# A fused attention, Fourier-mixing and expert kernel: raw weights loaded early, first factors on VectorE, a 127-row store cut in two, a list asked for later

## The chip, the cores and the metric

The kernel runs on one core of a Trainium2 chip. The metric is the device time of one execution in microseconds (us), from launch to end. The kernel before takes 1034.43 us, the median of 3 runs (1032.81 to 1038.68).

## The reference

The inputs are q, k, v of 4 sequences, 8 heads, 576 positions and 64 columns, and the weights of two later stages.

```
attn = softmax(q k^T / 8 - slope_h * |i - j|), only for 0 <= i - j < 128;  x = attn v -> (4, 576, 512)
u    = x + Re(FFT over the positions and over the 512 columns of x)
un   = (u - mean(u)) / sqrt(var(u) + 1e-6);  x2 = u + relu(un @ w_ch1) @ w_ch2      (512 -> 2048 -> 512)
each token of x2 picks an expert (argmax of a gate; a local gate may hand on the expert of the token before)
out  = p[e] * (relu(x2 @ w1[e]) @ w2[e])                                             (8 experts, 512 -> 1024 -> 512)
```

The two weights `w_ch1` and `w_ch2` are handed in as 64-bit floating-point words. The kernel reads them as pairs of 32-bit words and turns them into fp32 itself.

## The kernel before

All tokens lie in 18 groups of 128 rows (five to a sequence, the last one shared by two sequences). Every product of the two-layer networks is done in three fp32r matmuls (helper `mm3`, lines 161 to 164), with both factors split into a high and a low part: `split` (lines 157 to 159) copies the high part on ScalarE (ACT, line 158) and subtracts for the low part on VectorE (DVE) or GpSimd (POOL) (line 159).

The stages overlap on TensorE (PE):

- **Opening**, `opening()`: the attention of sequence 0, its Fourier mixing (`mixing(0)`) and the normalising of the first two groups, in an order written out by hand for PE, DVE, ACT and POOL.
- **First pass** over the first 1024 of the 2048 hidden columns (`mlp_first`, nine pairs of groups), with the attention and the mixing of sequences 1 to 3 beside it. Their pieces are laid on a time axis as lanes; behind that the framework's scheduler sets the order of each engine by its own estimates. Each engine, and SyncE's queue of DMAs (SP), then runs strictly in that order.
- **Second pass** over the other 1024 hidden columns, with the routing of tokens beside it (`route`, `assign`); during its last two pairs an early expert is begun for the 256 first tokens of the expert that leads so far (`early()`, `expert_weights(-1, e)`).
- **Experts**, eight of them, to the end.

`mixing(b)` ends in three steps. The first adds into `xs[0]` (lines 485 to 489) and stores two tiles to the DRAM tiles `ud`: 128 rows at line 492 and 127 rows at line 493 (the row that is left out comes in the third step, line 498). Lines 495, 496, 501 and 502 store the other rows. The tiles `xs` are a ring of four: the attention of a later sequence writes into them at line 401 when these stores have read them. `normalise` loads the groups back from `ud` (`u`, line 553), takes mean and variance on DVE (lines 558 and 560), works out 1/sqrt(var) in 12 tiny steps on POOL (lines 565 to 573: a power, then two Newton steps), scales on ACT (line 577), transposes on PE (line 511) and splits.

The weights of the two passes are converted chunk by chunk: a chunk is 256 hidden columns, in four raw pieces of 512 KB. `load_weights64` and `convert` take a raw piece `r` from a ring of two buffers (`RB = 2`, tag `r64`), load it on SP (line 228), scale it on ACT (line 232), put the words together in three DVE instructions (lines 233 to 235), and split. Four chunks belong to the first pass, four to the second. The third piece of a chunk thus waits in SP's queue until the first is converted.

In `early()`, the list of token slots (`ids`, line 981) is asked for one step after the first expert weights (`we`, line 940, also a ring of two `r64` buffers); it must wait until the last scatter into `slots` (POOL, line 867) has landed.

Of the kernel before, what the change touches and what calls it, by code (L numbers as in the profile page):

```python
# [52 lines left out]
TB_ = 3  # L53
WB = 3
FL = 2
EY = 8
EL = 7
HB = 4
VL = 3
# [91 lines left out]
def build(ctx, tc, a, out):  # L151
# [55 lines left out]
    def weight_tiles(wp):  # L207
        return (wp.tile([P, 2, 4, CB], F32R, tag="w1", name="t1"), wp.tile([P, 2, CB // P, DM], F32R, tag="w2", name="t2"))

    def load_weights64(tiles, w1, w2, c, words):  # L210
        t1, t2 = tiles
        q = CB // 2
        for j in range(2):
            f0 = c * CB + j * q
            s = w1[:, 2 * f0:2 * (f0 + q)].rearrange("(k p) f -> p k f", p=P)
            convert(t1[:, 0, :, j * q:(j + 1) * q], t1[:, 1, :, j * q:(j + 1) * q], s, words)
            yield
        for j in range(CB // P):
            f0 = c * CB + j * P
            s = w2[f0:f0 + P].rearrange("p (k f) -> p k f", k=4)  # L220
            convert(t2[:, 0, j].rearrange("p (k f) -> p k f", k=4), t2[:, 1, j].rearrange("p (k f) -> p k f", k=4), s, words)
            yield

    def convert(hi, lo, src, words):

        k, n = hi.shape[1], hi.shape[2]
        r = wraw.tile([P, k, 2 * n], U32, tag="r64", name="r64", bufs=RB)
        nc.sync.dma_start(out=r, in_=src)
        w = r.rearrange("p k (n t) -> p k n t", t=2)
        wl, y = w[:, :, :, 0], w[:, :, :, 1]  # L230
        t = words().rearrange("p (k n) -> p k n", k=k)
# [194 lines left out]
    def mixing(b):  # L426
        xs = xss.pop(b)
        rows = [(P, P), (P, P), (33, 32)]
        zin = []

        def fold(kt):
            n, m = rows[kt]
            xa, xb = xs[kt][:, 0], xs[kt][:, 1]
            xf = slab([P, 2, DM], F32, "xf", "m", MB)
            xe, xo = xf[:, 0], xf[:, 1]
            if kt == 0:

# [12 lines left out]
        zn = sm.tile([1, K1], F32, tag="tmp", name="zn", bufs=1)  # L450
        parts = ((1, 0), (1, 1), (0, 0)), ((0, 1), (0, 2))
        pss = {}

        def zprod(part, kt):
            xf, n = zin[kt]
            for cs, db in part:
                w = P if db < 2 else 1
                if kt == 0:
                    pss[cs, db] = ps_g.tile([P, DM], F32, tag="g", name="zps")
                nc.tensor.matmul(pss[cs, db][0:w, 0:K1], lhsT=xf[0:n, cs, db * P:db * P + w], rhs=tab1[0:n, cs, kt], start=kt == 0, stop=kt == 2)  # L460
                if kt == 2:
                    nc.scalar.copy(Z[cs][:, db] if db < 2 else zn, pss.pop((cs, db))[0:w, 0:K1])

        for kt in range(3):
            fold(kt)
            zprod(parts[0], kt)
            yield
        for kt in range(3):
            zprod(parts[1], kt)
        yield  # L470
        for kb in range(3):
            n = rows[kb][0]
            c0 = kb * P
            pc = ps_g.tile([P, DM], F32, tag="g", name="pc")
            pz = ps_g.tile([P, DM], F32, tag="g", name="pz")
            for cs, ps in ((1, pz), (0, pc)):
                for db in range(2):
                    nc.tensor.matmul(ps[0:n, 0:K2], lhsT=Z[cs][:, db, c0:c0 + n], rhs=tab2[:, cs, db], start=db == 0, stop=db == 1 and cs == 1)
            nc.tensor.matmul(pc[0:n, 0:K2], lhsT=zn[:, c0:c0 + n], rhs=alt, start=False, stop=True)
            cb_ = slab([P, 3, K2], F32, "cmb", "m", MB)  # L480
            sb, df, su = cb_[:, 0], cb_[:, 1], cb_[:, 2]
            nc.scalar.copy(sb[0:n], pz[0:n, 0:K2])
            nc.vector.tensor_tensor(out=df[0:n], in0=pc[0:n, 0:K2], in1=sb[0:n], op=ALU.subtract)
            nc.vector.tensor_tensor(out=su[0:n], in0=pc[0:n, 0:K2], in1=sb[0:n], op=ALU.add)
            for ab, lo, hi in ((0, df, su), (1, su, df)):
                m = rows[kb][ab]
                x = xs[kb][0:m, ab]
                nc.vector.tensor_tensor(out=x[:, 0:HN + 1], in0=x[:, 0:HN + 1], in1=lo[0:m, 0:HN + 1], op=ALU.add)
                nc.vector.tensor_tensor(out=x[:, DM - 1:HN:-1], in0=x[:, DM - 1:HN:-1], in1=hi[0:m, 1:HN], op=ALU.add)
            row = lambda t: ud[GIDX[b, t]]  # L490
            if kb == 0:
                nc.sync.dma_start(out=row(0), in_=xs[0][:, 0])
                nc.sync.dma_start(out=row(3)[1:P], in_=xs[0][1:P, 1])
            elif kb == 1:
                nc.sync.dma_start(out=row(1), in_=xs[1][:, 0])
                nc.sync.dma_start(out=row(2), in_=xs[1][:, 1])
            else:
# [4 lines left out]
                nc.sync.dma_start(out=um[r + 32:r + 64], in_=xs[2][0:32, 1])  # L502
            if kb == 2:
                mixed[0] = b
            yield
# [40 lines left out]
    def normalise(gs, xT, us, src=None):  # L546
# [15 lines left out]

        v = sm2.tile([P, 3, TM], F32, tag="v", name="v")
        v0, v1, v2 = (v[:, i, 0:n] for i in range(3))
        nc.gpsimd.tensor_scalar_add(v0, mv[:, 0:n, 1], 1.0e-6)
        nc.gpsimd.tensor_tensor(out=v1, in0=v0, in1=half[:, 0:n], op=ALU.pow)
        for _ in range(2):
            nc.gpsimd.tensor_tensor(out=v2, in0=v1, in1=v1, op=ALU.mult)
            nc.gpsimd.tensor_tensor(out=v2, in0=v2, in1=v0, op=ALU.mult)
            nc.gpsimd.tensor_scalar(out=v2, in0=v2, scalar1=-0.5, scalar2=1.5, op0=ALU.mult, op1=ALU.add)  # L570
            nc.gpsimd.tensor_tensor(out=v1, in0=v2, in1=v1, op=ALU.mult)
        nc.gpsimd.tensor_tensor(out=v2, in0=mv[:, 0:n, 0], in1=v1, op=ALU.mult)
        nc.gpsimd.tensor_scalar_mul(v2, v2, -1.0)
        yield
        for i, g in enumerate(gs):
            un = us[i]
# [37 lines left out]
                for _ in pre:  # L614
                    yield ("piece", 0)

    chunksA = [weight_tiles(wpA) for c in range(FA // CB)]
    def tables():

        with tc.issue_after(last["load"].ins):  # L620
# [14 lines left out]

    def conversions():
        for c in range(FA // CB):
            yield from load_weights64(chunksA[c], a["w_ch1"], a["w_ch2"], c, lambda: sm.tile([P, 2 * CB], U32, tag="t64", name="t64", bufs=2))

    END = object()  # L640

# [34 lines left out]
    def opening():  # L676

        for n, _ in enumerate(attention(0)):
            if n == 4:
                tables()  # L680
        attended.add(0)
        ends = [last[x].ins for x in ("x", "w", "pool")]
        xs = xss[0]
# [54 lines left out]
    chunksB = [weight_tiles(wpB) for c in range(FA // CB, FF // CB)]  # L738

    room = lact.tile([P, 4, 2 * CB], U32, tag="xTe", name="t64", bufs=1)  # L740
    turns = iter(range(4 * FF // CB))
    for c in range(FA // CB, FF // CB):
        for _ in load_weights64(chunksB[c - FA // CB], a["w_ch1"], a["w_ch2"], c, lambda: room[:, next(turns) % 4]):
            pass

    wt8 = late.tile([P, E], F32, name="wt8")
# [250 lines left out]
    def early():  # L997

        e = first_expert()
        pre_.add(expert_weights(-1, e))  # L1000
        yield
        x = slot_load(e * CAP, TM, 1)
        for _ in range(EL):
            yield
        ids[-1] = slot_ids(x, TM, 1)
        xTs[-1] = lact.tile([P, 2, 4, TM * P], F32R, tag="xTe", name="xTe", bufs=1)
# [196 lines left out]
```

## Time and profile before

| | |
|---|---|
| median of 3 runs | 1034.43 us |
| profiled execution, its time | 1039.1 us |
| its span, first to last instruction | 1037.4 us |
| PE busy | 946.8 us (91%) |
| DVE, ACT, POOL busy | 520.1, 381.3, 241.1 us |
| mean granted clock of PE | 0.959 |

Busy means that an instruction of the engine was running. The granted clock is the share of full speed that TensorE was allowed; 1.00 is 2.4 GHz and 0.50 is 1.2 GHz. Of the 1037.4 us, PE is idle in 90.6, and it runs at the lower of its two levels in several stretches beside these.

### The profile page before, as it was taken

Reading aid. Unit: us, or ns where it says so; the run is one execution under the profiler, and the core shown is the slowest. Engines: PE = TensorE matmul, PEld = TensorE weight load, DVE = VectorE, ACT = ScalarE, POOL = GpSimd, SP = SyncE. Lnnn points to the kernel's source line nnn. Section 1 sums busy time; section 2 is a strip of 40 time slices with the busy share of each in tenths; the row PEclk is TensorE's granted clock in tenths of the full one; section 3 lists DMA queues with packets and bytes.
Section 4 is the critical chain, followed back from the end, with each engine's and each line's share of the span. In section 5 each row is a group of like instructions: output and inputs, shape, how many; then the busy total and the mean of one; then the engine's idle time right before and its main releaser. Section 6 shows DMA issues by size and latency. Waiting matters only on the chain. (4 is left out here: it accounts for less than half of the span.)

```text
span 1037.4 us, 16275 instructions
## 1 busy us (share of the span) xinstructions
PE 946.8 (91%) x5959; PEld 770.6 (74%) x5959; DVE 520.1 (50%) x1286; ACT 381.3 (37%) x990; POOL 241.1 (23%) x358
## 2 busy tenths in 40 slices
PE   8877989889799888899999999997987999999993
PEld 4636666567568567688988888886876988888993
DVE  5777856636444455611133535354767644555510
ACT  5345654353252233421111111112436644454510
POOL 2245531230222034401011222222122212111100
PEclk9987999899989998999999999999999999999997
DMA  8345841342212155514344444444349745555300
GB/s 301 98 128 158 283 153 43 131 140 69 78 36 63 57 188 166 184 61 102 62 102 102 103 102 102 103 102 122 123 144 302 237 142 183 179 163 183 119 18 18
DMA packets 112103, 133.58 MB, mean 129 GB/s; under 512 B 16253, under 2 KB 79998, under 8 KB 111950
## 3 DMA queue, kind: packets, MB, share of 16 engines
q1 hardware_dynamic: 89166, 112.73, 34.0%
q0 software_dynamic: 22848, 19.72, 8.8%
q8 instruction: 49, 0.80, 0.3%
q14 instruction: 40, 0.33, 0.1%
HBM read 104.08 MB, written 31.23 MB: 130 GB/s over the span
## 5 line engine op out<-in xcount | busy, mean ns | idle before, releaser
L527 ACT ACTIVATE h<-hps 128x256 fp32r<-128x256 f32 x152 | 58.1, 382 | 263.7 <-PE hps L164 257.9
L528 DVE SCALAR_TENSOR_TENSOR h<-hps,h 128x256 fp32r<-128x256 f32 x152 | 63.7, 419 | 173.8 <-ACT h L527 173.5
L162 PE MATMUL acc<-t,h 128*128 128x512 f32 x304 | 127.8, 423 | 7.9 <-ACT h L527 7.0
L163 PE MATMUL acc<-t,h 128*128 128x512 f32 x304 | 123.6, 407 | 0.9 <-POOL t L159 0.8
L164 PE MATMUL acc<-t,h 128*128 128x512 f32 x304 | 120.5, 400 | 0.5 <-DVE h L528 0.5
L159 DVE TENSOR_TENSOR t<-we,t 128x512 fp32r<-128x512 f32 x144 | 93.8, 686 | 53.0 <-ACT t L158 52.3
L158 ACT CAST t<-we 128x512 fp32r<-128x512 f32 x144 | 82.6, 618 | 49.7 <-PE acc L164 24.9
L162 PE MATMUL hps<-xT,t 128*128 128x256 f32 x288 | 87.9, 305 | 4.9 <-DVE h L528 2.8
L162 PE MATMUL hps<-xTe,t 128*128 128x256 f32 (+5 forms) x288 | 87.0, 303 | 2.3 <-ACT xTe L158 2.3
L163 PE MATMUL hps<-xTe,t 128*128 128x256 f32 (+5 forms) x288 | 86.7, 301 | 0.3 <-DVE xTe L159 0.3
L164 PE MATMUL hps<-xTe,t 128*128 128x256 f32 (+5 forms) x288 | 86.9, 302 | 0.0
L164 PE MATMUL hps<-xT,t 128*128 128x256 f32 x288 | 84.4, 293 | 0.2 <-POOL t L159 0.2
L163 PE MATMUL hps<-xT,t 128*128 128x256 f32 x288 | 84.1, 292 | 0.0
L162 PE MATMUL hps<-xTb,t 128*128 128x256 f32 x288 | 83.2, 289 | 0.0
L164 PE MATMUL hps<-xTb,t 128*128 128x256 f32 x288 | 82.6, 287 | 0.0
L163 PE MATMUL hps<-xTb,t 128*128 128x256 f32 x288 | 82.2, 286 | 0.0
L345 ACT ACTIVATE t<-t,mx 128x128 f32<-128x128 f32 (+1 forms) x160 | 62.6, 394 | 47.3 <-DVE mx L338 43.1
L162 PEld LDWEIGHTS acc<-t,h 128*128 128x128 f32 x304 | 58.1, 193 | 25.5 <-ACT h L527 11.9
L162 PEld LDWEIGHTS hps<-xT,t 128*128 128x128 f32 x288 | 57.6, 200 | 16.1 <-DVE h L528 7.6
L162 PE MATMUL acc<-t,hE 128*128 128x512 f32 x168 | 67.6, 402 | 0.1
L164 PEld LDWEIGHTS acc<-t,h 128*128 128x128 f32 x304 | 57.7, 191 | 12.6 <-DVE h L528 1.1
L163 PEld LDWEIGHTS acc<-t,h 128*128 128x128 f32 x304 | 58.8, 194 | 10.3 <-POOL t L159 2.3
(260 smaller groups left out, 2039.8 us busy)
## 6 DMA issues: line engine op xcount, KB each, us to landing
we<-in_w SPq DMA_DIRECT2D x72, 512.0 KB
r<-in_w_ch SPq DMA_DIRECT2D x32, 512.0 KB
qkt<-in_qk SPq DMA_DIRECT2D x15, 642.0 KB
nd<-xT SPq DMA_DIRECT2D x18, 512.0 KB
xTb<-nd POOLq DMA_DIRECT2D x18, 512.0 KB, 6.0
vt<-in_v SPq DMA_DIRECT2D x16, 384.0 KB
pd<-y SPq DMA_DIRECT2D x18, 256.0 KB
ub<-ud SPq DMA_DIRECT2D x18, 256.0 KB
```

The lines of the kernel that those rows point to most:

```text
L158: nc.scalar.copy(hi, src)
L159: (eng or nc.vector).tensor_tensor(out=lo, in0=src, in1=hi.bitcast(F32), op=ALU.subtract)
L162: nc.tensor.matmul(o, lhsT=wh, rhs=xh, start=start, stop=False, **kw)
L163: nc.tensor.matmul(o, lhsT=wh, rhs=xl, start=False, stop=False, **kw)
L164: return nc.tensor.matmul(o, lhsT=wl, rhs=xh, start=False, stop=stop, **kw)
L345: nc.scalar.activation(t[0:m, j], t[0:m, j], AF.Exp, bias=mx[0:m, j:j + 1], scale=-1.0, accum_out=sums[0:m, j:j + 1])
L527: nc.scalar.activation(h[:, 0, 0:n], hps[:, 0:n], AF.Relu)
L528: nc.vector.scalar_tensor_tensor(out=h[:, 1, 0:n], in0=hps[:, 0:n], scalar=0.0, in1=h[:, 0, 0:n].bitcast(F32), op0=ALU.max, op1=ALU.subtract)
```

## The change

Four edits:

1. **Raw weights.** `load_raw` loads the four raw pieces of a chunk into the place of a chunk that is not converted yet (tiles `rw` with the tags `w1` and `w2` of the weights' own pool). Chunks 0 to 2 of each pass go that way, chunk 3 still goes through the ring `r64`. In the opening chunk 0 is asked for after step 9 of the attention, chunks 1 and 2 after step 14; in the second pass chunks 4 to 6 behind the last store to `ud`. A chunk is then converted from its raw tile, into the tile that is free next.
2. **First factors.** Where `normalise` gets its rows from SBUF (only the first pair of groups, in the opening), 1/sqrt is worked out on DVE: a bit-shift first guess and three Newton steps, 17 tiny instructions in place of POOL's 12.
3. **Stores.** The 127-row store becomes one of 112 rows and one of 15.
4. **Early list.** The list `ids` is asked for seven steps later, behind the first weights; it is read two steps after that, and the rows are transposed five (`EY`) and not eight steps after they are gathered: 15 steps in all, 16 before.

```diff
-EY = 8
+EY = 5
...
+    def blocks64(c):
...
+            yield w1[:, 2 * f0:2 * (f0 + q)].rearrange("(k p) f -> p k f", p=P)
...
+            yield w2[f0:f0 + P].rearrange("p (k f) -> p k f", k=4)
+
+    def load_raw(c, wp=None):
+        if wp is not None:
+            raws[c] = [x[:, i] for x in (wp.tile([P, 2, 4, CB], U32, tag=g, name="rw") for g in ("w1", "w2")) for i in range(2)]
+        for i, s in enumerate(blocks64(c)):
+            if wp is None:
+                raws.setdefault(c, []).append(wraw.tile([P, 4, CB], U32, tag="r64", name="r64", bufs=RB))
+            nc.sync.dma_start(out=raws[c][i], in_=s)
+            yield
+
+    def load_weights64(chunks, i, c, wp, words):
+        t1, t2 = chunks[i] = weight_tiles(wp)
+        q = CB // 2
+        late_load = load_raw(c) if c not in raws else iter(())
+        for _ in range(RB - 1):
+            next(late_load, None)
+        for i in range(4):
+            next(late_load, None)
+            r = raws[c][i]
...
-                nc.sync.dma_start(out=row(3)[1:P], in_=xs[0][1:P, 1])
+                nc.sync.dma_start(out=row(3)[1:P - 15], in_=xs[0][1:P - 15, 1])
+                nc.sync.dma_start(out=row(3)[P - 15:P], in_=xs[0][P - 15:P, 1])
...
+        eng = nc.gpsimd if src is us else nc.vector
+        eng.tensor_scalar_add(v0, mv[:, 0:n, 1], 1.0e-6)
+        if src is us:
+            eng.tensor_tensor(out=v1, in0=v0, in1=half[:, 0:n], op=ALU.pow)
+        else:
+            r = v1.bitcast(I32)
+            eng.tensor_single_scalar(r, v0.bitcast(I32), 1, op=ALU.logical_shift_right)
+            eng.tensor_scalar(out=r, in0=r, scalar1=-1.0, scalar2=float(0x5F3759DF), op0=ALU.mult, op1=ALU.add)
+        for _ in range(2 if src is us else 3):
...
...
             if n == 4:
                 tables()
+            if n == 9:
+                for _ in load_raw(0, wpA):
+                    pass
+            if n == 14:
+                for c in range(1, nA - 1):
+                    for _ in load_raw(c, wpA):
+                        pass
...
+    with tc.issue_after(last["ud"].ins):
+        for c in range(nA, nA + nB - 1):
+            for _ in load_raw(c, wpB):
+                pass
...
         pre_.add(expert_weights(-1, e))
         yield
+        for _ in range(EL):
+            yield
         x = slot_load(e * CAP, TM, 1)
-        for _ in range(EL):
+        for _ in range(2):
             yield
```

The built orders below carry line numbers of their own program; in the changed one, 513 to 516 are the stores 492 and 493, 576 is the load of `u`, 254 to 256 are 233 to 235, 608 is 577, 982 is 940, 1023 is 981, 1106 is 1062 and 1073 is 1029.

SP's queue in the mixing of sequence 2, before (`ud` and `u` as above, `x` the tile that is stored):

```order
L492 DMA ud_70<-x 128x512
L493 DMA ud_73<-x 127x512
L553 DMA u<-ud_70 128x512
L495 DMA ud_71<-x 128x512
L496 DMA ud_72<-x 128x512
```

And in the changed kernel:

```order
L513 DMA ud_70<-x 128x512
L515 DMA ud_73<-x 112x512
L516 DMA ud_73<-x 15x512
L576 DMA u<-ud_70 128x512
L518 DMA ud_71<-x 128x512
L519 DMA ud_72<-x 128x512
```

Nothing changes its place; the load of `u` stands behind the two parts as it stood behind the one.

DVE in the opening, from the last variance to the words `t_861` of a raw piece, before (`cmb` and `x` are the third step of the mixing, `s` and `t` scores of sequence 1):

```order
L560 BN_AGGR mv<-st 128x2
L483 TENSOR_TENSOR cmb<-pc,cmb 33x257
L484 TENSOR_TENSOR cmb<-pc,cmb 33x257
L488 TENSOR_TENSOR x<-x,cmb 33x257
L489 TENSOR_TENSOR x<-x,cmb 33x255
L488 TENSOR_TENSOR x<-x,cmb 32x257
L489 TENSOR_TENSOR x<-x,cmb 32x255
L233 TENSOR_SCALAR t_861<-r_859 128x512
L336 SCALAR_TENSOR_TENSOR t<-s,bias 65x512
L234 SCALAR_TENSOR_TENSOR t_861<-r_859,t_861 128x512
L338 TENSOR_REDUCE mx<-t 65x4
L235 SCALAR_TENSOR_TENSOR t_861<-r_859,t_861 128x512
```

The end of the same stretch in the changed kernel (`v` are the factors, `t_873` the words of the raw piece):

```order
L603 TENSOR_TENSOR v<-mv,v 128x2
L604 TENSOR_SCALAR v<-v 128x2
L504 TENSOR_TENSOR cmb<-pc,cmb 33x257
L505 TENSOR_TENSOR cmb<-pc,cmb 33x257
L509 TENSOR_TENSOR x<-x,cmb 33x257
L510 TENSOR_TENSOR x<-x,cmb 33x255
L509 TENSOR_TENSOR x<-x,cmb 32x257
L510 TENSOR_TENSOR x<-x,cmb 32x255
L254 TENSOR_SCALAR t_873<-rw 128x512
L255 SCALAR_TENSOR_TENSOR t_873<-rw,t_873 128x512
L256 SCALAR_TENSOR_TENSOR t_873<-rw,t_873 128x512
```

The 17 factor instructions, and one COPY_PREDICATED of 128x512 among them, now stand ahead of the third mixing step and of the words. On ACT the order at this place is the same in both: the CAST of these words, and behind it the scaling of `u`.

SP's queue around the early list, before:

```order
L940 DMA we<-in_w 128x4x256
L940 ISA
L940 DMA we<-in_w 128x2x512
L1029 DMA p__6882<-pd_94 128x512
L1062 DMA x2d<-x_7156 128x512
L1029 DMA p__6887<-pd_95 128x512
L981 ISA
L981 DMA ids<-slots_115 128x2x4
L940 ISA
L940 DMA we<-in_w 128x4x256
```

And in the changed kernel, from the third load of weights on:

```order
L982 DMA we<-in_w 128x4x256
L1073 DMA p__6884<-pd_95 128x512
L982 ISA
L982 DMA we<-in_w 128x2x512
L1106 DMA x2d<-x_7154 128x512
L982 ISA
L982 DMA we<-in_w 128x4x256
L1023 ISA
L1023 DMA ids<-slots_115 128x2x4
```

The list stood third behind two loads of weights; it now stands behind five.

## Rows read from the trace of the kernel before

**Rows 1.** The page, its first line.
```profile
span 1037.4 us, 16275 instructions
```
**Rows 2.** Timeline of SP's queue: start, us, DMA; mixing of sequence 2.
```profile
266.79 0.25 SPq L493 DMA_DIRECT2D ud<-x  x1
268.24 3.07 SPq L553 DMA_DIRECT2D u<-ud  x1
```
**Rows 3.** Windows: length, busy us (count) by engine, granted clock, DMA share, GB/s.
```profile
276.00:280.00 4.00, 0.25 (x3) 0.01 (x1) 0.00 (x0) 0.00 (x0) 0.00 (x0) 1.00 0.06 24
280.00:284.00 4.00, 1.14 (x16) 0.97 (x16) 3.79 (x11) 0.00 (x0) 2.23 (x8) 0.59 0.18 69
284.00:288.00 4.00, 2.45 (x6) 0.83 (x7) 1.04 (x3) 2.84 (x9) 1.33 (x5) 0.50 0.47 161
288.00:292.00 4.00, 4.00 (x10) 1.84 (x9) 1.50 (x5) 1.45 (x8) 1.02 (x3) 0.50 0.00 0
292.00:296.00 4.00, 4.00 (x16) 2.54 (x16) 1.61 (x4) 0.15 (x1) 0.00 (x0) 0.70 0.16 37
```
**Rows 4.** Timeline of DVE; idle before it and its releaser in brackets.
```profile
280.18 0.69 DVE L558 BATCH_NORM_STATS2 st<-u 128x6 f32<-128x512 f32 x1 [10.76 <-DMA u<-ud]
```
**Rows 5.** Timeline of PE, same place.
```profile
281.89 1.14 PE L373 MATMUL o<-w,vt 128*64 128x65 f32 x16 [5.64 <-DVE cmb L484]
```
**Rows 6.** Timeline of DVE, mixing of sequence 1.
```profile
194.92 0.42 DVE L401 TENSOR_TENSOR x<-xps,rec 128x256 f32<-128x256 f32 x1 [3.79 <-DMA ud<-x]
```
**Rows 7.** Timeline of PE, same place.
```profile
195.40 1.12 PE L354 MATMUL pt<-ident,t 128*128 128x128 f32 x4 [2.25 <-DVE x L401]
198.28 1.98 PE L373 MATMUL o<-w,vt 128*64 128x128 f32 x16 [1.77 <-POOL sums L346]
```
**Rows 8.** Windows, same place.
```profile
190.00:200.00 10.00, 5.98 (x52) 4.41 (x48) 4.31 (x10) 2.90 (x12) 2.79 (x5) 0.77 0.37 124
200.00:210.00 10.00, 7.62 (x48) 5.44 (x44) 4.60 (x11) 4.68 (x19) 3.39 (x14) 0.89 0.28 100
```
**Rows 9.** Timeline of SP's queue, early list.
```profile
719.86 0.39 SPq L981 DMA_DIRECT2D ids<-slots  x1
720.52 1.02 SPq L940 DMA_DIRECT2D we<-in_w  x2
```
**Rows 10.** Waits of SP's queue, whole run: us in total, times, longest.
```profile
SPq L981 <- DMA slots<-ent,su: 10.2, 4, 6.1
```
**Rows 11.** Timeline of ACT, same place.
```profile
724.26 1.14 ACT L158 CAST t<-we 128x512 fp32r<-128x512 f32 x2 [9.10 <-DMA we<-in_w]
725.30 0.36 ACT L791 COPY lt<-lps 10x256 f32<-10x256 f32 x1
```
**Rows 12.** Timeline of PE, same place.
```profile
725.72 0.38 PE L795 MATMUL pn<-ident,lt 10*128 10x10 f32 x2 [6.43 <-ACT lt L791]
```
**Rows 13.** Windows, same place.
```profile
724.00:728.00 4.00, 2.29 (x7) 1.87 (x8) 3.09 (x9) 2.82 (x6) 0.43 (x1) 0.56 0.52 186
728.00:732.00 4.00, 4.00 (x21) 3.56 (x20) 1.63 (x15) 1.03 (x4) 1.83 (x2) 0.59 0.97 295
```
**Rows 14.** Timeline of ACT in the opening.
```profile
73.62 0.60 ACT L158 CAST t<-t 128x512 fp32r<-128x512 f32 x1
75.48 0.81 ACT L577 ACTIVATE u<-x,v 128x512 f32<-128x512 f32 x1 [1.26 <-POOL v L573]
82.07 0.65 ACT L232 ACTIVATE r<-r 128x512 f32<-128x512 f32 x1 [3.27 <-DMA r<-in_w_ch]
```
**Rows 15.** Timeline of DVE in the opening.
```profile
72.73 0.67 DVE L235 SCALAR_TENSOR_TENSOR t<-r,t 128x512 uint32<-128x512 uint32 x1
```
**Rows 16.** Timeline of DVE: two tiny steps, one on the other's result.
```profile
763.98 0.16 DVE L1128 TENSOR_SCALAR eid<-eid 1x8 int32<-1x8 int32 x1
764.17 0.15 DVE L1129 TENSOR_REDUCE most<-eid 1x1 int32<-1x8 int32 x1
```
**Rows 17.** Waits of PE from 364 to 416 us, where the second weights are converted.
```profile
PE tps L511 <- ACT u L577: 5.1, 2, 3.4
```

More of the change, by code (lines that the diff above doesn't have):

```diff
@@ L208, in weight_tiles @@
         return (wp.tile([P, 2, 4, CB], F32R, tag="w1", name="t1"), wp.tile([P, 2, CB // P, DM], F32R, tag="w2", name="t2"))
-    def load_weights64(tiles, w1, w2, c, words):
-        t1, t2 = tiles
+    raws = {}
+    def blocks64(c):
+        w1, w2 = a["w_ch1"], a["w_ch2"]
         q = CB // 2
@@ L214, in load_weights64, with convert @@
             f0 = c * CB + j * q
-            s = w1[:, 2 * f0:2 * (f0 + q)].rearrange("(k p) f -> p k f", p=P)
-            convert(t1[:, 0, :, j * q:(j + 1) * q], t1[:, 1, :, j * q:(j + 1) * q], s, words)
-            yield
+            yield w1[:, 2 * f0:2 * (f0 + q)].rearrange("(k p) f -> p k f", p=P)
         for j in range(CB // P):
             f0 = c * CB + j * P
-            s = w2[f0:f0 + P].rearrange("p (k f) -> p k f", k=4)
-            convert(t2[:, 0, j].rearrange("p (k f) -> p k f", k=4), t2[:, 1, j].rearrange("p (k f) -> p k f", k=4), s, words)
-            yield
[L224 to L228, printed above, removed]
+            yield w2[f0:f0 + P].rearrange("p (k f) -> p k f", k=4)
[6 more added lines that the diff above has]
+            nc.sync.dma_start(out=raws[c][i], in_=s)
+            yield
+    def load_weights64(chunks, i, c, wp, words):
[7 more added lines that the diff above has]
+            r = raws[c][i]
+            if i < 2:
+                convert(t1[:, 0, :, i * q:(i + 1) * q], t1[:, 1, :, i * q:(i + 1) * q], r, words)
+            else:
+                convert(t2[:, 0, i - 2].rearrange("p (k f) -> p k f", k=4), t2[:, 1, i - 2].rearrange("p (k f) -> p k f", k=4), r, words)
+            yield
+    def convert(hi, lo, r, words):
         w = r.rearrange("p k (n t) -> p k n t", t=2)
         wl, y = w[:, :, :, 0], w[:, :, :, 1]
-        t = words().rearrange("p (k n) -> p k n", k=k)
+        t = words().rearrange("p (k n) -> p k n", k=4)
         nc.scalar.activation(y.bitcast(F32), y.bitcast(F32), AF.Copy, scale=BIAS)
@@ L501, in mixing @@
                 nc.sync.dma_start(out=um[r:r + 32], in_=xs[2][0:32, 0])
-                nc.sync.dma_start(out=um[r + 32:r + 64], in_=xs[2][0:32, 1])
+                last["ud"] = nc.sync.dma_start(out=um[r + 32:r + 64], in_=xs[2][0:32, 1])
             if kb == 2:
@@ L564, in normalise @@
         v0, v1, v2 = (v[:, i, 0:n] for i in range(3))
[L565 to L573, printed above, removed]
+        eng = nc.gpsimd if src is us else nc.vector
+        eng.tensor_scalar_add(v0, mv[:, 0:n, 1], 1.0e-6)
+        if src is us:
+            eng.tensor_tensor(out=v1, in0=v0, in1=half[:, 0:n], op=ALU.pow)
+        else:
+            r = v1.bitcast(I32)
+            eng.tensor_single_scalar(r, v0.bitcast(I32), 1, op=ALU.logical_shift_right)
+            eng.tensor_scalar(out=r, in0=r, scalar1=-1.0, scalar2=float(0x5F3759DF), op0=ALU.mult, op1=ALU.add)
+        for _ in range(2 if src is us else 3):
+            eng.tensor_tensor(out=v2, in0=v1, in1=v1, op=ALU.mult)
+            eng.tensor_tensor(out=v2, in0=v2, in1=v0, op=ALU.mult)
+            eng.tensor_scalar(out=v2, in0=v2, scalar1=-0.5, scalar2=1.5, op0=ALU.mult, op1=ALU.add)
+            eng.tensor_tensor(out=v1, in0=v2, in1=v1, op=ALU.mult)
+        eng.tensor_tensor(out=v2, in0=mv[:, 0:n, 0], in1=v1, op=ALU.mult)
+        eng.tensor_scalar_mul(v2, v2, -1.0)
         yield
@@ L615, in mlp_first @@
                     yield ("piece", 0)
-    chunksA = [weight_tiles(wpA) for c in range(FA // CB)]
+    chunksA = [None] * nA
     def tables():
@@ L637, in conversions @@
         for c in range(FA // CB):
-            yield from load_weights64(chunksA[c], a["w_ch1"], a["w_ch2"], c, lambda: sm.tile([P, 2 * CB], U32, tag="t64", name="t64", bufs=2))
+            yield from load_weights64(chunksA, c, c, wpA, lambda: sm.tile([P, 2 * CB], U32, tag="t64", name="t64", bufs=2))
     END = object()
@@ L737, in build @@
     lact = c2.enter_context(pool("lact", 2, reuse_waits="tile"))
-    chunksB = [weight_tiles(wpB) for c in range(FA // CB, FF // CB)]
+    chunksB = [None] * nB
     room = lact.tile([P, 4, 2 * CB], U32, tag="xTe", name="t64", bufs=1)
     turns = iter(range(4 * FF // CB))
+    with tc.issue_after(last["ud"].ins):
+        for c in range(nA, nA + nB - 1):
+            for _ in load_raw(c, wpB):
+                pass
     for c in range(FA // CB, FF // CB):
-        for _ in load_weights64(chunksB[c - FA // CB], a["w_ch1"], a["w_ch2"], c, lambda: room[:, next(turns) % 4]):
+        for _ in load_weights64(chunksB, c - nA, c, wpB, lambda: room[:, next(turns) % 4]):
             pass
```

## The prediction

> **What bounds the kernel now.** I read the page first: the span is 1037.4 us [rows 1] in an execution of 1039.1 us, so 1.7 us lie around it, and that execution is 4.7 us above the median of the three runs, 1034.43. PE is busy in 946.8 us of the span. It is in-order, and its work is not changed, so time can come only from its 90.6 us of idle time and from the stretches in which its granted clock lies at the lower level. Next I listed PE's waits by window, to see who ends them, and then, at each long one, read the timelines of PE, of its releaser and of SP's queue until something stood there that the change touches. Three places answer.
>
> The first is the mixing of sequence 2. SP issues the 127-row store at 266.79 and the load of `u` at 268.24 [rows 2]. From 276 to 280 us DMA moves 24 GB/s at a share of 0.06 [rows 3]: that is one of 16 engines (1/16 = 0.0625) and nothing else. 127 rows of 2 KB are 254 KB, at 24 GB/s 10.6 us. So this store runs on one engine, and whatever needs all 16 engines and is issued behind it lands behind it: `u` reaches DVE at 280.18 after DVE has sat idle for 10.76 us [rows 4]. The mixing's next additions stand behind this instruction on DVE, and PE waits 5.64 us for them [rows 5]. The second place is the same store in the mixing of sequence 1: there DVE waits 3.79 us to write over a tile that is still being stored [rows 6], and PE waits 2.25 and 1.77 us behind it [rows 7]. The third is the early list: SP stands still for up to 6.1 us until the last scatter has landed [rows 10], asks for the list at 719.86 and only then for more weights at 720.52 [rows 9]; the CAST of these waits on ACT for 9.10 us, the copy `lt` stands behind it [rows 11], and PE waits 6.43 us for `lt` [rows 12].
>
> **Part by part. The stores.** In the mixing of sequence 2, PE is idle from 276 to 288 us for 3.75 + 2.86 + 1.55 = 8.2 us (4.00 less its busy time in three windows), and then works with the clock low: 1.14, 2.45, 4.00 and 4.00 us at 0.59, 0.50, 0.50 and 0.70 [rows 3]. At full clock that work would take the busy time by the clock, 6.7 us, so the low clock costs 11.6 - 6.7 = 4.9. Together 13.1 us. With 112 rows on more than one engine, `u` can land about 11 us sooner, before PE's wait begins at 276; the order of PE and DVE is the same there. What is late next is small: scores and exponentials that PE waited for anyway. I take 12 of the 13.1, bounded by 8 (some of the waits stay, and the clock falls for part of the stretch) and 13.
>
> In the mixing of sequence 1 the two waits are 4.0 us [rows 7]. The low clock costs 5.98 x 0.23 + 7.62 x 0.11 = 2.2 [rows 8]. I take 6 of the 6.2, bounded by 3 and 8 (the low part may cost more than a mean over 10 us shows).
>
> No row shows a store of 112 or of 15 rows. The nearest rows bound them: if 15 rows, 30 KB, also went by one engine at 24 GB/s, they would take 1.3 us; if the 112 rows did too, 224 KB would take 9.3 us and the gain would be gone (a rival, below). The Trainium skill has a rule for it ("DMA: Bandwidth & Descriptors", section "Why a DMA increments its semaphore by 16 and not by 1"): a DMA uses the largest number of engines up to 16 that divides its slowest dimension. By that, 127 rows have one engine, 112 have 16, 15 have 15, and the sum would be the one I take; the share of 0.06 agrees for the 127, and no run here shows the others.
>
> **The early list.** It now stands behind five loads of weights. The third load needs only its buffer, free when the first piece is split; a piece reaches ACT 3.7 us after its issue (720.52 to 724.26, [rows 9, 11]). ACT has been free for its CAST since 724.26 - 9.10 = 715.2, and PE comes to its wait at 725.72 - 6.43 = 719.3, so the piece has four us in which to come and be cast unnoticed; I take it that it does, and the 6.43 us go [rows 12]. Behind the wait PE runs at 0.56 and 0.59: 2.29 x 0.44 + 4.00 x 0.41 = 2.6 us [rows 13]. Together 9.1. The list itself cannot come sooner: the scatter it waits for is not moved, so it is still asked for near 720. But DVE's reading of it now stands in the middle of the routing, and PE's transposes of the gathered rows come 9 us earlier, and 18 matmuls earlier in PE's order. Queued behind DVE's reading are a routing product and the splits of weights; PE waits for both. I count 2 us of new waits, bounded by 0 and 6 (the 6.1 of [rows 10] moved whole to another place). That leaves 7, from 3 to 9.
>
> **First factors on DVE.** The factors end on POOL just before ACT starts on `u` at 75.48 [rows 14]. On DVE, a tiny step follows the one it depends on by 0.19 us (763.98 to 764.17, [rows 16]): 17 steps are 3.3 us, and with the instructions that stand between they would be ready about 1.8 us sooner than now. It does not help. On ACT a CAST stands ahead of `u`; it started at 73.62 [rows 14], because the last DVE instruction for it ended at 72.73 + 0.67 = 73.40 [rows 15]. That instruction now has the 17 steps and one more pass (as long as the one of [rows 15], 0.67) in front of it: it ends at 73.4 + 3.3 + 0.7 = 77.4, and `u` starts near 78.0, 2.5 us later than now.
>
> **Raw weights, opening.** Against that, ACT's wait of 3.27 us for a raw piece at 82.07 [rows 14] goes: the pieces have landed by then, and no 127-row store is in front of them. It delayed the second cast of the first pair by about 2.5 us beyond its turn. Net for the opening 0, bounded by -3 (a loss: the ten scalings that now stand ahead of the mixing's first copies on ACT, and scores of sequence 1 that PE does later) and +3 (PE is idle and its clock low here, so what goes counts twice). SP passes 6 MB of raw pieces before sequence 1's q and k; these are needed only when sequence 0's attention is over, so I cost that at nothing.
>
> **Raw weights, second pass.** From 364 to 416 us PE waits 5.1 us for scaled rows [rows 17], behind POOL's factors, raw pieces on ACT and the last 127-row store. With the raw loads no longer tied to the conversion, ACT and DVE no longer wait for pieces in front of work for PE; but the scheduler has laid this stretch anew, and seven of the twelve loads stand behind stores of `y` on SP. I take 3, bounded by -4 (the loads come late and the last conversions with them) and +8 (these waits and the low clock around them go).
>
> **Sum.** 12 + 6 + 7 + 0 + 3 = 28 us: 1039.1 - 28 = 1011.1 for the profiled execution, and 1034.4 - 28 = 1006.4 against the median. I forecast 1006. With all lower bounds the gain is 8 + 3 + 3 - 3 - 4 = 7 (1027), with all upper ones 13 + 8 + 9 + 3 + 8 = 41 (993).
>
> **Rivals.** *Only the stores count.* The list's wait moves from SP to DVE and to PE's transposes: PE gets there 9 us sooner and waits for rows whose gather depends on a scatter that is no sooner. For it: the list is bound to the scatter. Against it: the present schedule has the rows gathered well ahead of their transposes. Time: 1034.4 - (12 + 6 + 0 + 0 + 1) = 1015.
>
> *The stores don't do what they say.* Either part still goes by one engine, and the 18 us stay. For it: no row shows another row count near 112. Against it: all other stores of 128 rows land in a few us. Time: 1034.4 - 10 = 1024.
>
> *The conversions free more.* If the second pass gives its 8 and the opening 3, 1034.4 - (12 + 6 + 7 + 3 + 8) = 998. For it: PE's waits there are all for engines that themselves waited for raw pieces. Against it: the tiny factor steps stay on POOL there.
>
> *Slower.* ACT now has ten scalings ahead of the first copies of the mixing's products, and the last two need pieces of chunk 3, which SP asks for behind a load of values that waits for a buffer. If those pieces came late, ACT, the mixing and everything behind would shift by as much. It decides against the change only from the point where the copies come more than 28 us late; at 32 us the time would be 1034.4 - 28 + 32 = 1038. For it: the queue is crowded there, with 6 MB of raw pieces in front. Against it: a piece needs 3.7 us from issue to ACT [rows 9, 11], and even the one that stands behind a 127-row store keeps ACT for only 3.27 us [rows 14].
>
> **Chances.** A measurement of this kernel tells about 0.5%, 5 us, from no change. Forecast (1000 to 1012) 0.52; stores only (to 1020) 0.18; conversions free more (below 1000) 0.12; stores fail (1020 to 1029) 0.08; within 5 us 0.05; slower 0.05. The range of 8 in 10 runs from 993 to 1021. Faster 0.90, same 0.05, slower 0.05.
>
> **What would show it.** Stores: no stretch of 10 us at a DMA share of 0.06 behind the mixing, DVE's wait for `u` near 270 under 3 us, PE at full clock through the mixings of sequences 1 and 2. List: no wait of PE for `lt`; the list still asked for when the scatter lands; a wait of PE at the transposes of the gathered rows at most 3 us. Factors: ready sooner, and `u` nevertheless scaled later than the factors allow, behind the CAST. Raw weights: no wait of ACT for a raw piece before 130 us. I am wrong if a part of the store still crawls on one engine, if PE's idle time in the mixings comes back under another releaser, or if ACT's first copies wait for raw pieces.

## The result

The changed kernel takes 1020.88 us, the median of 4 runs (1018.75 to 1026.44), against 1036.56 us for the kernel before in the same rounds (median of 4, 1032.81 to 1042.31). The ratio is 0.9844, 95% interval 0.9801 to 0.9887: about 16 us less, where the forecast was 28. Run again later beside another set of the kernel before, it gave 0.9845 (0.981 to 0.9879). The profiled execution took 1018.75 us.

### The profile page after: what moved, and what is told of

The parts are those of the page before. It is cut to its first block, busy times and chain, and to the rows that moved or that the text cites. A ratio compares the mean times of both kernels' runs of the same rounds, so it can differ in the third digit from the quotient of the medians.

```text
span 1017.0 us, 16257 instructions
## 1 busy us (share of the span) xinstructions
PE 933.0 (92%) x5958; PEld 765.9 (75%) x5959; DVE 523.8 (51%) x1303; ACT 382.1 (38%) x990; POOL 236.5 (23%) x346
```

## The profile after

The first lines of the page, the second with busy time, share and instructions of each engine, answer to [rows 1]:

```profile
span 1017.0 us, 16257 instructions
PE 933.0 (92%) x5958; PEld 765.9 (75%) x5959; DVE 523.8 (51%) x1303; ACT 382.1 (38%) x990; POOL 236.5 (23%) x346
```

PE's idle time fell from 90.6 to 84.0 us, only 6.6 us; the other 13.8 of the span's 20.4 us are a higher clock while it works (946.8 to 933.0 busy).

*Stores, mixing of sequence 2.* SP's queue (start, us, DMA), which answers to [rows 2]; DVE's reading of `u`, to [rows 4]; windows as in [rows 3]:

```profile
262.00 0.33 SPq L515 DMA_DIRECT2D ud<-x  x1
262.38 0.46 SPq L516 DMA_DIRECT2D ud<-x  x1
263.45 0.34 SPq L576 DMA_DIRECT2D u<-ud  x1
```
```profile
266.16 0.69 DVE L581 BATCH_NORM_STATS2 st<-u 128x6 f32<-128x512 f32 x1 [1.53 <-DMA u<-ud]
```
```profile
263.00:267.00 4.00, 4.00 (x30) 3.29 (x29) 2.44 (x7) 2.68 (x11) 1.13 (x3) 1.00 0.44 123
271.00:275.00 4.00, 3.27 (x31) 1.57 (x29) 1.44 (x3) 3.64 (x12) 1.48 (x4) 1.00 0.46 166
```

`u` is there 2.7 us after its load is asked for, not 11.9; DVE waits 1.53 us in place of 10.76, PE's wait of 5.64 us [rows 5] is gone, and the clock stays at 1.00.

*Stores, mixing of sequence 1.* A window that answers to the first of [rows 8]; PE's waits of [rows 7] are gone, and PE is busy throughout:

```profile
186.00:196.00 10.00, 10.00 (x93) 6.63 (x90) 7.81 (x19) 5.03 (x20) 3.86 (x8) 1.00 0.58 190
```

*Early list.* PE's timeline, which answers to [rows 12], and windows, to [rows 13]:

```profile
705.06 0.29 PE L837 MATMUL pn<-ident,lt 10*128 10x10 f32 x2 [0.30 <-ACT lt L833]
709.19 0.38 PE L864 MATMUL tp<-ident,oh 128*8 128x128 f32 x2 [1.07 <-DVE rmx L855]
710.77 0.59 PE L864 MATMUL tp<-ident,oh 128*8 128x128 f32 x2 [0.97 <-DVE oh L859]
```
```profile
708.00:712.00 4.00, 1.96 (x10) 1.39 (x9) 2.57 (x17) 1.53 (x4) 0.47 (x1) 0.84 0.77 256
712.00:716.00 4.00, 4.00 (x20) 3.50 (x19) 4.00 (x13) 1.53 (x3) 1.57 (x2) 0.73 0.65 197
```

The wait for `lt` fell from 6.43 to 0.30 us, but two waits of a microsecond follow, and behind them the clock falls to 0.84 and 0.73.

*Opening.* DVE, the last instruction of the first factors; ACT, which answers to [rows 14] (the first row is a wait that was not there before); and PE:

```profile
73.70 0.17 DVE L604 TENSOR_SCALAR v<-v 128x2 f32<-128x2 f32 x1
```
```profile
49.77 0.69 ACT L253 ACTIVATE r<-r 128x512 f32<-128x512 f32 x1 [3.86 <-DMA r<-in_w_ch]
77.74 0.62 ACT L158 CAST t<-t 128x512 fp32r<-128x512 f32 x1 [5.64 <-DVE t L256]
78.27 0.81 ACT L608 ACTIVATE u<-x,v 128x512 f32<-128x512 f32 x1
```
```profile
79.13 1.11 PE L534 MATMUL tps<-ident,u 128*128 128x128 f32 x4 [8.26 <-ACT u L608]
```

The factors are ready at 73.87, `u` is scaled at 78.27 behind the CAST, and PE waits 8.26 us for it (2.56 us in the trace of before).

*Second pass.* First what PE waits for where the second weights are converted (to [rows 17]); then DVE, POOL and ACT there; last a window of 13 us:

```profile
368.87 0.55 PE L534 MATMUL tps<-ident,u 128*128 128x128 f32 x3 [4.24 <-ACT u L608]
383.46 0.58 PE L162 MATMUL hps<-xT,t 128*128 128x256 f32 x1 [3.47 <-DVE h L551]
401.39 0.80 PE L162 MATMUL acc<-t,h 128*128 128x512 f32 x1 [4.40 <-ACT h L550]
```
```profile
377.87 1.51 DVE L254 TENSOR_SCALAR t<-rw 128x512 uint32<-128x512 uint32 x1 [1.47 <-POOL t L159]
379.41 1.65 DVE L255 SCALAR_TENSOR_TENSOR t<-rw,t 128x512 uint32<-128x512 uint32 x1
380.99 1.48 DVE L254 TENSOR_SCALAR t<-rw 128x512 uint32<-128x512 uint32 x1
382.39 0.68 DVE L256 SCALAR_TENSOR_TENSOR t<-rw,t 128x512 uint32<-128x512 uint32 x1
382.99 0.41 DVE L551 SCALAR_TENSOR_TENSOR h<-hps,h 128x256 fp32r<-128x256 f32 x1
```
```profile
376.53 5.66 POOL L159 TENSOR_TENSOR t<-t,t 128x512 fp32r<-128x512 f32 x4 [8.56 <-ACT t L158]
393.19 0.30 POOL L590 TENSOR_SCALAR v<-mv 128x2 f32<-128x2 f32 x1 [2.35 <-DVE mv L583]
...
394.36 0.48 POOL L599 TENSOR_TENSOR v<-v 128x2 f32<-128x2 f32 x1
...
396.95 1.26 POOL L159 TENSOR_TENSOR t<-t,t 128x512 fp32r<-128x512 f32 x1
...
399.28 0.23 POOL L604 TENSOR_SCALAR v<-v 128x2 f32<-128x2 f32 x1
```
```profile
399.55 1.52 ACT L608 ACTIVATE u<-u,v 128x512 f32<-128x512 f32 x2 [5.64 <-POOL v L604]
400.97 0.36 ACT L550 ACTIVATE h<-hps 128x256 fp32r<-128x256 f32 x1
```
```profile
377.00:390.00 13.00, 9.53 (x55) 8.50 (x54) 12.07 (x14) 7.26 (x15) 8.51 (x7) 0.87 0.11 38
```

The first of the three waits comes ahead of the bunch; where it stands, PE waited 1.79 and 1.43 us in the trace of before. Then the raw pieces are all there, so the conversion comes in a bunch: DVE is busy 12.07 of 13 us. Four subtractions on POOL run one behind the other, and three passes over the words on DVE, beside them, take 1.5 to 1.65 us each. Without a subtraction beside it, a pass like the second takes 0.67 [rows 15], one like the first and third (line 254) 0.41 us, as in the opening at 75.78 us. The second half of `h` stands behind these passes, and PE waits 3.47 us for it. Later the factors take POOL 6.3 us (393.19 to 399.51), a split among them; `u` waits on ACT, the next `h` behind `u`, and PE 4.40 us for that.

## The experiments

All ratios are to the kernel before in the same rounds. As one execution differs from the next by some 5 us, I also compared positions: for each instruction of PE that both programs have, how much earlier it starts than in the profiled execution of the kernel before (median over the instructions near each time of before, us):

```
us in the trace of before       60    155    240    310    480    675    742    880
full change, first profile    -0.3   -0.4    4.8   17.0   15.3   16.0   19.6   20.7
full change, second profile   -0.8    2.1    7.4   19.6   17.6   18.0   23.6   24.4
stores alone                  -0.9    3.9    9.0   21.3   21.4   21.8   23.3   25.9
list alone                    -0.3    1.5    1.2    1.9    2.0    2.1    7.7    7.3
opening alone                 -0.9    1.6    1.7    2.0    3.9    3.6    4.9    5.7
113 and 14 rows               -1.3   -0.2    0.7    1.2    2.2    2.5    4.4    5.1
126 and 1 rows                -1.0    4.0    9.4   21.6   23.3   24.2   25.2   26.1
stores + list                 -1.0    3.2    8.2   20.4   20.6   21.2   27.3   24.2
stores + list, again          -1.0    3.8    8.8   21.0   21.6   22.2   28.3   26.0
... + raw weights, opening    -1.6    2.9    8.1   20.3   23.0   23.5   29.5   29.1
... + factors                 -1.3    0.0    5.2   17.5   17.6   18.2   23.5   21.1
... + raw weights, 2nd pass   -1.4    3.4    9.1   21.3   15.5   16.0   22.1   22.0
all but raw weights, 2nd p.   -4.2   -4.2    1.1   13.6   12.6   12.9   17.0   16.0
```

What a stage gives is the difference of two columns. Differences of about 2 us in a stage, and up to 3 us behind 742, also occur between programs with the same order there. The rows with "..." are stores + list and what is named; the last row lost 3 us more than its like in its first 60 us, where its order is that of the full change (from 38 to 46 us its clock is 0.57). A profiled execution need not lie at its kernel's median: it took 1014.27 us in the second profile of the full change (median 1020.77), 1009.97 with the raw weights of the opening (1014.09) and 1022.63 in the last row (1017.86).

**Stores alone.**

```diff
-                nc.sync.dma_start(out=row(3)[1:P], in_=xs[0][1:P, 1])
+                nc.sync.dma_start(out=row(3)[1:P - 15], in_=xs[0][1:P - 15, 1])
+                nc.sync.dma_start(out=row(3)[P - 15:P], in_=xs[0][P - 15:P, 1])
```

> The kernel before with the one edit that the 127-row store becomes 112 and 15 rows; every engine's order stays as before. Theory A (the parts add, and what a part saves is kept): TensorE's instructions come about 5 us earlier after the mixing of sequence 1 and 12 us more after that of sequence 2, as they do in the changed kernel, and these 17 us are kept to the end: about 17 us below the kernel before, ratio 0.984; no idle time of TensorE above 2 us in the two mixings, and the granted clock 0.98 or more from 276 to 296 us. Rival B (the second pass takes back what was saved ahead of it, whatever stands in it, because its rows and weights come no earlier): 17 us ahead at 350 us, and 3 to 7 us of this lost between 360 and 440 us: 10 to 14 us below, ratio 0.987 to 0.990.

1014.51 us, ratio 0.9785 (0.9758 to 0.9813): 22 us less, more than the full change gives and 5 more than theory A has. 5.1 us come in the mixing of sequence 1 (3.9 to 9.0), 12.3 in that of sequence 2 (9.0 to 21.3), and none is lost in the second pass: rival B falls. The third piece is in the opening, from -0.9 to 3.9 at 155 us, where the list alone, with the same opening as before, goes from -0.3 to 1.5: some 3 us. ACT's raw piece behind the 3.27 us wait of [rows 14] is scaled at 79.63 now, without a wait (first fence); PE's wait in the trace of before for the cast `xT` that stands behind that piece on ACT (second fence) is gone:

```profile
79.63 0.67 ACT L232 ACTIVATE r<-r 128x512 f32<-128x512 f32 x1
```
```profile
83.25 0.58 PE L162 MATMUL hps<-xT,t 128*128 128x256 f32 x1 [2.00 <-ACT xT L158]
```

**113 and 14 rows, 126 and 1 row.**

```diff
-                nc.sync.dma_start(out=row(3)[1:P], in_=xs[0][1:P, 1])
+                nc.sync.dma_start(out=row(3)[1:P - 14], in_=xs[0][1:P - 14, 1])
+                nc.sync.dma_start(out=row(3)[P - 14:P], in_=xs[0][P - 14:P, 1])
```

(1 for 14 in the other kernel.)

> The kernel before with the 127-row store cut in 113 and 14 rows in place of 112 and 15. Theory A (the number of engines must divide the row count, and 113 is prime; after the Trainium skill, DMA: Bandwidth & Descriptors, Why a DMA increments its semaphore by 16 and not by 1): the 113 rows, 226 KB, go by one engine at 24 GB/s in about 9.4 us; a stretch of DMA at a share of 0.06 stands behind the mixing of sequence 2 again, VectorE waits 8 us or more for u there, and the time is like before, 1033 to 1036 us, ratio 0.996 to 1.0. Rival B (it is the cut in two, or a full row count of 127, that matters): like 112 and 15 rows, 1014.5 us, ratio 0.9785.

> The kernel before with the 127-row store cut in 126 rows and 1 row. Theory A (a divisor of the row count up to 16 sets the engines: 14 for 126): like 112 and 15 rows, 1012 to 1017 us, ratio 0.977 to 0.981, and no stretch of DMA at a share of 0.06 longer than 1 us in the mixing of sequence 2. Rival B (the row count must be a multiple of 16 to leave the one engine): like before, 1034 to 1037 us, ratio 0.998 to 1.0.

113 and 14 rows: 1032.26 us, 0.9964 (0.9946 to 0.9982). 126 and 1: 1014.41 us, 0.9815 (0.9778 to 0.9852). Two windows of the first, DVE there, and DVE in the second:

```profile
273.00:274.00 1.00, 1.00 (x10) 0.88 (x10) 0.00 (x0) 0.00 (x0) 0.00 (x0) 1.00 0.06 25
277.00:278.00 1.00, 0.00 (x0) 0.00 (x0) 0.00 (x0) 0.00 (x0) 0.00 (x0) 1.00 0.06 25
```
```profile
278.47 0.69 DVE L559 BATCH_NORM_STATS2 st<-u 128x6 f32<-128x512 f32 x1 [9.71 <-DMA u<-ud]
```
```profile
261.57 0.69 DVE L559 BATCH_NORM_STATS2 st<-u 128x6 f32<-128x512 f32 x1 [1.51 <-DMA u<-ud]
```

With 113 rows the DMA share is 0.06 again, one engine of 16, at 25 GB/s, and `u` lands behind it; with 126 rows DVE waits 1.51 us. So neither the cut in two nor a multiple of 16 matters. By the divisor rule that the forecast weighed (the Trainium skill, "DMA: Bandwidth & Descriptors", section "Why a DMA increments its semaphore by 16 and not by 1"), 113 rows have 1 engine and 126 have 14. The 113 rows agree with it by their share; the 126 rows don't go by one engine, but that it is 14 no view here shows.

**List alone.**

```diff
-EY = 8
+EY = 5
...
+        for _ in range(EL):
+            yield
         x = slot_load(e * CAP, TM, 1)
-        for _ in range(EL):
+        for _ in range(2):
```

> The kernel before with the early list's edit alone (list asked for seven steps later, read two steps after that, transposes five steps after the gathers). Theory A: TensorE's wait of 6.4 us for the copy lt goes, and two waits of about 1 us each for the one-hot rows come in its place with some low clock: 4 to 5 us below the kernel before, ratio 0.995. Rival B, the forecast's size: the low clock behind the wait goes too and nothing comes in its place: 7 us or more, ratio 0.993. Rival C: the wait only moves to the transposes of the gathered rows: within 1 us of before.

1032.31 us, 0.9969 (0.9945 to 0.9993): 3 us. By position it gains 5.6 us between 675 and 742, where kernels without this edit show 1.0 to 1.9 too: 4 us. B's 7 us lie outside the interval. Here also the wait for `lt` is gone and a smaller loss stands nearby (one PE row, two windows):

```profile
713.19 0.65 PE L511 MATMUL tps<-ident,x 128*128 128x128 f32 x4 [1.17 <-DVE x L1063]
```
```profile
712.00:716.00 4.00, 2.42 (x11) 1.73 (x11) 4.00 (x8) 2.58 (x6) 1.59 (x2) 0.89 0.65 213
716.00:720.00 4.00, 4.00 (x25) 2.94 (x23) 2.63 (x4) 2.12 (x5) 2.37 (x2) 0.68 0.63 202
```

Theory A holds in kind, a little under its 4 to 5 us by the times; the two waits for the one-hot rows are not in this kernel but one for `x`, so the place of the new waits depends on the rest.

**Opening alone, and its two edits apart.** "Opening alone" is before with `load_raw(0, wpA)`, `load_raw(1)`, `load_raw(2)` in the attention and the factors on DVE. The two apart were added to stores + list:

```diff
 factors:              +        eng = nc.gpsimd if src is us else nc.vector   (all instructions of the factors on eng)
 raw weights, opening: +                for _ in load_raw(c, wpA): pass       (c = 0 at step 9, 1 and 2 at step 14)
```

> The kernel before with the raw weights of the first pass loaded early and the first factors on VectorE; stores, list and second pass as before. Theory A: the first scaling of u on ScalarE starts 2 to 3 us later than before (78 against 75.5), since it stands behind a cast that waits for VectorE; ScalarE's wait for raw pieces goes; by 150 us TensorE is within 1 us of the kernel before, and so is the end: ratio 0.999 to 1.001. Rival B: without the 127-row store's delay in this kernel taken away (it stays here) the raw pieces behind it still cost nothing, and the freed ScalarE gains 3 us, ratio 0.997. Rival C: the later u costs its 2.5 us to the end, ratio 1.0025.

> Stores and list as changed, the first factors on VectorE; all raw loads as before. Theory A (the 17 tiny steps stand ahead of the words on VectorE, and the first u behind the cast of these): u is scaled about 78 us and not near 76, TensorE comes to the transposes 2 to 2.5 us later, and the end is 2 to 3 us above stores and list alone. Rival B (the first factors were the opening's bound): u is scaled 1 to 2 us sooner and the end is 1 to 3 us below.

> Stores and list as changed, raw weights of the first pass loaded early, the first factors on GpSimd as before, second pass as before. It differs from the run without the second pass's early raw loads (1017.9 us) in the factors alone, and from stores and list alone in the opening's raw loads alone. Theory A (the factors on VectorE cost: 17 tiny steps stand ahead of the words, these ahead of a cast, the cast ahead of u): u is scaled at 76 to 77 us and not at 78.3, and the time is 2.5 to 5 us below 1017.9, near that of stores and list alone: ratio 0.976 to 0.979. Rival B (the early raw loads cost, since ScalarE's scalings and the new order of sequence 1's attention go with them): like 1017.9, ratio 0.981.

Opening alone: 1039.2 us, 1.0027 (1.0000 to 1.0054), a small loss if any: B falls, A and C stay open. By position it shows no loss, but its profiled execution, 1033.16 us, is one of its fastest. Though the 127-row store is whole here, ACT has no wait for a raw piece between 54 and 130 us: the early loads alone end the 3.27 us wait of [rows 14] too. Factors with stores and list: 1016.88 us, 0.9794 (0.9759 to 0.983), 2.5 us above stores and list of the same rounds; by position 1.3 us are gained up to 155 us where stores and list gain 4.2 to 4.8. (With the store cut, the four profiles with the factors on DVE gain -0.1 to 2.9 us up to there, the six with the factors on POOL 4.2 to 5.0.) ACT and PE with the factors on DVE, and on POOL (stores + list, again):

```profile
79.31 0.81 ACT L585 ACTIVATE u<-x,v 128x512 f32<-128x512 f32 x1
```
```profile
80.17 1.12 PE L512 MATMUL tps<-ident,u 128*128 128x128 f32 x4 [8.27 <-ACT u L585]
```
```profile
76.49 0.81 ACT L578 ACTIVATE u<-x,v 128x512 f32<-128x512 f32 x1 [1.25 <-POOL v L574]
```
```profile
77.36 0.90 PE L512 MATMUL tps<-ident,u 128*128 128x128 f32 x3 [2.55 <-ACT u L578]
```

The first `u` is 2.8 us later, PE waits 8.27 us for it, not 2.55, and comes to its transposes 2.8 us later (80.17 against 77.36): theory A. Raw weights with stores and list: 1014.09 us, 0.9801 (0.9776 to 0.9826), by position 4.5 up to 155 us, as without them. The two measures don't agree on a loss of 2 us; neither A nor B is shown, and what these loads cost stays open.

**Raw weights of the second pass: taken from the full change, and added to stores and list.**

```diff
-    with tc.issue_after(last["ud"].ins):
-        for c in range(nA, nA + nB - 1):
-            for _ in load_raw(c, wpB):
-                pass
```

> The changed kernel without the early raw loads of the second pass: its weights go through the ring of two raw buffers again. Theory A (the early raw pieces let the conversion come in a bunch: VectorE is busy 12 of 13 us from 377 to 390 us and the words, slowed beside GpSimd's subtractions, stand ahead of the second halves of h, of xT and of the statistics): without them VectorE is busy at most 8 of any 13 us before 395 us, TensorE's waits of 4.2, 3.5 and 4.4 us between 364 and 403 us are halved, and the time is 1.5 to 4 us below the changed kernel: ratio to before 0.979 to 0.981. Rival B (TensorE waits there because it comes 17 us earlier than what feeds it, with or without the raw loads): time like the changed kernel's or up to 4 us above, ratio to before 0.983 to 0.988.

> Stores and list as changed, and the early raw loads of the second pass; opening as before, first factors on GpSimd. Theory A (the early raw pieces let the second conversion bunch: VectorE full, GpSimd's factor steps slowed, TensorE waits for u and h): TensorE's positions lose 3 to 7 us against stores and list alone between 380 and 440 us and get part of it back; the end is 2 to 5 us above stores and list alone. Rival B (raw pieces that wait for nothing free ScalarE and VectorE, as the forecast has it): 0 to 3 us below stores and list alone.

Taken out: 1017.86 us, 0.9811 (0.9786 to 0.9835), 3 us below the full change (0.9844), with intervals that overlap. Added: 1017.11 us, 0.9808 (0.9772 to 0.9845), 3.9 us above stores and list (0.9770) of the same rounds. The positions tell the two groups apart. From 365 to 480 us, the stretch in question, the three profiles with these loads lose 2.0, 2.2 and 3.1 us; the ten without lie between 0.0 and a gain of 2.5, 1.5 where the loads are taken out. (Between 310 and 480 us the table has 5.8 for the kernel with the loads added, and a loss of 1.0 for the one with them taken out: each has lost 2.5 to 2.7 us before the stretch, in 7 us, from 318 and from 325 us on, in which its clock is 0.52.) The 13 us in question in both kernels, added and not:

```profile
377.00:390.00 13.00, 9.53 (x51) 8.37 (x51) 12.76 (x15) 7.26 (x15) 8.52 (x7) 0.87 0.15 43
```
```profile
377.00:390.00 13.00, 9.37 (x50) 7.81 (x48) 7.19 (x11) 5.46 (x10) 6.12 (x13) 0.87 0.39 122
```

DVE is busy 12.76 us with the loads and 7.19 without. PE waits 4.24, 3.47 and 4.39 us with them, for the same three things as in the full change; without, nothing above 1.69 but one wait of 3.63. Theory A holds and rival B falls, by the positions in both. One thing stays open: the scheduler lays the engines' orders anew when the loads are moved, and no run here moves the loads and keeps the orders. With the loads taken out PE's longest waits there are 1.62, 1.78 and 3.30 us. DVE is fuller there than theory A has it (10.9 of the 13 us from 352.5 us on, not 8 at most), and it has one full window, but later, and PE is busy and at full clock in it:

```profile
404.00:417.00 13.00, 12.50 (x76) 10.12 (x75) 11.83 (x19) 8.19 (x16) 5.37 (x4) 1.00 0.80 251
```

**Stores and list, a version that beats both.**

> The kernel before with the cut store (112 and 15 rows) and the early list's edit, nothing else. Theory A (parts add): 21.9 us by the stores alone and 3 to 4 by the list alone, so 24 to 26 us below before, about 1011 us, ratio 0.975 to 0.977, and 8 to 11 us below the full change: the raw loads and the first factors together cost that. Rival B (the list's gain shrinks once the stores' gain is there): like the stores alone, 1014 to 1015 us, ratio 0.9785.

> Stores and list alone, run once more beside the full change on one chip. Theory A (the raw loads and the first factors together cost 7 to 8 us, as the ratios 0.9772 and 0.9844 of separate rounds say): 1011 to 1014 us, 6 to 9 us below the full change of the same rounds. Rival B (that difference is scatter between rounds): within 3 us of the full change.

> The full change, run once more. Theory A: 1019 to 1022 us, ratio 0.984 to 0.986. Rival B (its first four runs were high by chance): 1013 to 1016 us, ratio 0.978 to 0.980.

Stores and list: 1012.46 us, 0.9772 (0.9738 to 0.9805), and again 1013.25, 0.9770 (0.9736 to 0.9804). The full change beside the latter: 1020.77, 0.9845 (0.981 to 0.9879). The two runs side by side are as theory A has it, and B falls: the raw loads and the factors together cost 7 to 8 us. The first run of stores and list does not decide between its own A and B, since B's 0.9785 lies within the interval: whether the list adds anything to the stores by itself (0.9771 against 0.9785) the times don't tell.

## Why the forecast was right in sign and its gain 12 us too large

- **Stores, +18.** Right in cause, and in size at both places: 5.2 + 12.2 = 17.4 us by position in the full change, against 6 + 12. `u` lands sooner, no long stretch at a share of 0.06 is left, the clock is full. What failed is what the forecast left out here: the store of the first mixing held up the raw piece of [rows 14], which the forecast named ("even the one that stands behind a 127-row store") and then credited to the raw loads.
- **Opening, 0.** The net was about right (-0.1 and 2.9 up to 155 us, against 1.8 in the list alone), its terms were not what they were given to. The factors do what was forecast: ready at 73.9, and `u` nevertheless at 78.27 behind the CAST, 2.8 us late; that costs 2.5 us by the times. Some 3 us pay for it, from ACT's wait that goes. But either edit ends that wait alone: the cut store (stores alone) and the raw loads (opening alone). Joined, it counts once, and with the store cut the raw loads add nothing (4.5 up to 155 us, as without them). Beside the cut store, then, the opening's two edits give nothing and cost at least what the factors cost. "No ACT wait for a raw piece before 130 us" was wrong by the 3.86 us at 49.77; ACT had waited for PE there before, so it cost nothing.
- **Early list, +7.** The wait of 6.43 us goes, as forecast. The step that failed is the sum of what comes in its place: 2 us of new waits were counted, and no clock behind them. In the full change PE's waits between 696 and 716 us in this part are 3.6 us, and the low clock costs 1.96 x 0.16 + 4.00 x 0.27 = 1.4: 9.1 - 3.6 - 1.4 = 4.1, where the positions give 3.6 (5.6 in the second profile; 1.0 to 1.9 of such a figure kernels without this edit show too).
- **Raw weights, second pass, +3.** Wrong in sign: a loss of 2 to 3 us by position, where kernels without these loads gain 0 to 2.5; about -4 by the times. The step that failed is "ACT and DVE no longer wait for pieces in front of work for PE". Those waits had also spread the conversion over time. Without them DVE fills up, its passes and POOL's subtractions hold each other up, and `h` and the factors stand behind them. That POOL and DVE stretch each other is shown by the rows: DVE's passes take 1.5 to 1.65 us beside a subtraction, 0.68 or less without, and POOL's tiny steps 0.48 beside DVE's passes, 0.23 without. The Trainium skill has a rule that fits ("SBUF — State Buffer", section "SBUF: two separate sides"): the two engines share a pair of ports, and an instruction of VectorE that is in a mode with two ports, or has two inputs in SBUF while GpSimd reads there, does not hold it together with one of GpSimd; the one that starts first has it for the whole instruction, the other blocks. Of the three slow passes the second has two inputs; whether the other two ran in such a mode no view here shows, and no run took that contention away alone.
- **Sum.** By the times: stores 22, list 1 to 3, second pass -4, factors -2.5, raw loads of the opening -2 to 0, so 14 to 19; measured 16. Against that, the forecast was 4 us too small for the stores, 4 to 6 too large for the list, 7 for the second pass and 2.5 to 4.5 for the opening. Luck has a share in it: errors of both signs met, and 1020.88 lies only just inside the range of 993 to 1021. Of the rivals, "only the stores count" came nearest in gain (19 us), for other reasons: the list did gain by itself, and the conversions, which it had at +1, lost. The band in which the time lies, 1020 to 1029, was given to "the stores fail", and that is not what happened: by themselves they gave 22.

## What to carry to other kernels

Look at the row count of every store ahead of a load that something waits for: the stores of 127 and of 113 rows, which no number from 2 to 16 divides, went by one engine at 24 to 25 GB/s, and the load behind them landed late; 112 + 15 and 126 + 1 rows did not, and no run shows a cost of the second store. A wait that is removed from an engine off the critical path may have been what kept its work spread out; before it goes, look at what then stands ahead of the critical engine's suppliers. And when two edits end the same wait, it counts once: here the cut store alone gave more than the whole change, and its gain hid what the others cost.

## What was not expected of the hardware

The clock of one stretch of one program differs from execution to execution. The full change twice, the same program, two windows in the first pass, the first profile and then the second:

```profile
104.00:110.00 6.00, 5.30 (x17) 4.31 (x18) 4.08 (x7) 3.01 (x12) 3.44 (x3) 0.50 0.00 0
122.00:128.00 6.00, 5.16 (x25) 4.20 (x25) 4.67 (x10) 2.41 (x8) 2.67 (x3) 0.72 0.93 303
```
```profile
104.00:110.00 6.00, 4.00 (x26) 3.27 (x25) 4.68 (x9) 4.35 (x15) 3.46 (x3) 1.00 0.00 0
122.00:128.00 6.00, 5.85 (x50) 4.49 (x51) 5.57 (x12) 3.86 (x13) 3.80 (x6) 1.00 1.03 380
```

PE had the same waits ahead of the first window in both, the longest 2.03 us, and got 1.2 GHz in one execution and 2.4 in the other. By position the first execution falls 3.6 us behind the second from 104 to 132 us, and 2.5 of that is left between the two at 155 us. A gain of 3 us near such a place can't be read from one profile.
